# A fused RWKV-5 attention and SoLU block: zeros, own products, scalings and one join on other engines or in another order, and the decay rates loaded as eight rows

## The chip, the cores and the metric

The kernel runs on one core of a Trainium2 chip. Times are device microseconds (us) of one execution. A core has five engines that run side by side: TensorE (PE, with its weight loads shown apart as PEld), VectorE (DVE), ScalarE (ACT), GpSimd (POOL) and SyncE (SP), which here does nothing but issue transfers. Each works through its own instructions in the order in which they were written, and waits for another only through semaphores. Sixteen DMA engines move data between the device's memory and the on-chip buffers SBUF and PSUM.

## What is computed

The first part is a linear attention with a decaying state, over 4 batches, 8 heads, 768 steps and 48 columns to a head; the second a feed-forward block with the activation SoLU on its 3072 rows.

```python
# attention: r, k, v (4, 8, 768, 48); w, u (8, 48)
for t in range(S):
    cur = einsum('bhd,bhe->bhde', u[None] * k_t, v_t)
    y[:, :, t] = einsum('bhd,bhde->bhe', r_t, state + cur)
    state = w[None, :, :, None] * state + einsum('bhd,bhe->bhde', k_t, v_t)
# x: y as (4*768, 8*48); w_in (384, 1024), w_out (1024, 384)
h = x @ w_in
solu = h * softmax(h)
ln = (solu - mean(solu)) / sqrt(var(solu) + 1e-6) * g_ln
out = ln @ w_out
```

The weights w_in, w_out and g_ln are read in single precision or as the words of doubles, which the kernel turns into single precision itself ("convert" below).

## The kernel before

The 768 steps of each batch are cut into six chunks of 128, so there are 24 units of 128 rows, taken batch by batch within a chunk: unit i is batch i mod 4 of chunk i // 4. A unit goes through the attention, then through w_in (two units later, `LA`), and then through w_out (five units after that, `LO`). The order of the instructions on every engine is the order of the program text: `direct_path` turns automatic scheduling off. The other path in the file, `general_path`, is only taken when a check at the end (decay rates and sums within bounds) fails.

**The start.** SP issues the loads of k, r, v and of the pieces of w_in in the written order (lines 594 to 608). ACT's queue carries only two small loads, w (L493) and u (L496). The 8 x 48 decay rates go to four rows of `wq`, with two heads in each, padded with ones to 64 columns, and PE turns them into `wd_ps`, 128 x 4 (L636). From these DVE builds the powers in `tab` by doubling: `back` and `fore`. PE turns `back` into `kd_ps`, and ACT copies that to `kdec` (L665), the factors of the keys. u goes to one row, and PE spreads it over 128 rows through `u_ps`, which ACT copies to `u_bc` (L639). Right behind that copy ACT fills the second half of each of the six v buffers with zeros (L641), 128 x 512 each.

Then a list written out by hand (lines 1313 to 1396) brings in the first units. `turn_r` and `turn_k` turn r and k by PE; DVE multiplies with `fore` (L779) and, for unit 0, with `back` (L790). `decay_k` is POOL's product of k and kdec (L721). `weigh` forms u times k (L734) and times r (L735), both on POOL, and DVE's `sum_own` (L739) adds these up to the own term of each row and head. `diagonal` puts that on the diagonal of the score matrix: for the first four units ACT does so in eight pieces (L749), for the later ones POOL (L754). `take_scores` is DVE's masked copy of the scores from PSUM (L827, later L832); `whole_y`, `merged_y` are PE's products with v. `spin` is a filler product of PE. The state is advanced by `outer` and `whole_outer` (PE), `middle` and `update` (DVE).

**The pieces of the weights.** There are 14: six of w_in and eight of w_out. `convert_a` (ACT, L537), `convert_b` (two operations of DVE, L550 and L552) and `convert_c` (POOL, L560) build the single-precision words. `convert_d` multiplies a piece of w_out with the negative of g_ln: on ACT if the flag `scalar` is set (L568), else on DVE (L571). In the loop of lines 1399 to 1448 the odd pieces go to ACT and the even ones to DVE. In each of its passes the order on ACT is: exponential of `h_ps` (L977), copy of the turned keys, `convert_a`, the two operations of `unit_b`, `convert_d`, then (in the last two passes) `halve_ln`, `place` (L771, L772), the copy of y (`take_y`, L892). On DVE it is: `turn_r`'s product (L779), `unit_a` (L1049, L1053, which reads h_ps and so frees it), `convert_d`, the own sums, state, scores, and `convert_b`.

**The feed-forward.** `ffn_in` multiplies with w_in (L969). `unit_a` forms solu, `unit_b` the sum of squares. `variance`, `root` and `shifts` make the two numbers to a row with which `normalise` (ACT, L1102) scales a unit. `halve_ln` splits the words into halves of 16 bits, SP transposes them by DMA (L1116), and DVE's `join_ln` joins the halves again (L1121). `row_sums_12` and `row_sums_34` (L1201 to L1207) form sums for a scheme that needs seven products where eight are usual; `both_a` to `both_d` are its products with w_out (L1211) and the copies of their results. At the end the last unit's `shifts` run on DVE, between two joins:

```python
    both_c(l)
    shifts(i, N, nc.vector)
    join_ln(l + 3)
    row_sums_12(l + 2)
```

Of the kernel before, what the change touches and what calls it, by code (L numbers as in the profile page):

```python
# [9 lines left out]
F32 = mybir.dt.float32  # L10
# [389 lines left out]
def direct_path(  # L400
# [29 lines left out]
    nc = tc.nc  # L430
    B, H, S, D = r.shape
    T = 128
    P = U = 64
    C = S // T
    HP = H // 2
# [13 lines left out]
    const = ctx.enter_context(tc.tile_pool(name="const", bufs=1))  # L449
    apool = ctx.enter_context(tc.tile_pool(name="apool", bufs=2))  # L450
# [15 lines left out]
    NLD, NV = 5, 6  # L466
    rpads = [const.tile([128, H, P], F32, name=f"rpad{i}") for i in range(NLD)]
    kpads = [const.tile([128, H, P], F32, name=f"kpad{i}") for i in range(NLD)]
    vts = [const.tile([128, 2, H, P], F32, name=f"vt{i}") for i in range(NV)]
# [12 lines left out]
                    in_=v[b, :, ds(c * T + at, size), :].rearrange("h s d -> s h d"))  # L482


    wq = const.tile([HP, 2, P], F32, name="wq")
    u_bc = const.tile([128, H, D], F32, name="u_bc")
    g_sb = const.tile([128, KF], F32, name="g_sb")
    minus_g = const.tile([128, KF], F32, name="minus_g")
# [1 line left out]
    w_out_sb = const.tile([128, KF, dm], F32, name="w_out_sb")  # L490
    decays = const.tile([128, HP], F32, name="decays")

    nc.scalar.dma_start(out=wq[:, :, 0:D], in_=w.rearrange("(a q) d -> a q d", q=2))  # L493
    nc.vector.memset(wq[:, :, D:], 1.0)
    u_row = u_bc[0:1].rearrange("p h d -> p (h d)")
    nc.scalar.dma_start(out=u_row, in_=u.rearrange("h d -> (h d)").unsqueeze(0))  # L496
    for i in range(NLD):
# [42 lines left out]
    def convert_b(j):  # L540
        hi, low = step[j]
        n = low.shape[1]
        ma = wpool.tile([128, n], U32, tag="ma", name="ma", bufs=4)
        part = ma
        if pieces[j][2] is None:
            part = psM.tile([128, n], F32, tag="m", name="part").bitcast(U32)

        nc.vector.tensor_scalar(out=part, in0=hi, scalar1=3, scalar2=0x3FFFFFF8,  # L550
                                op0=ALU.logical_shift_left, op1=ALU.bitwise_and)
        nc.vector.scalar_tensor_tensor(out=ma, in0=hi, scalar=0xC0000000, in1=part,  # L552
                                       op0=ALU.bitwise_and, op1=ALU.bitwise_or)
        step[j] = ma, low
# [8 lines left out]
    def convert_d(j, scalar=False):  # L563
        dst, _, f = pieces[j]
        ma, low = step.pop(j)
        if f is not None:
            if scalar:
                nc.scalar.activation(out=dst, in_=ma.bitcast(F32), func=ACT.Copy,  # L568
                                     scale=minus_g[:, f : f + 1])
            else:  # L570
                nc.vector.tensor_scalar_mul(out=dst, in0=ma.bitcast(F32),  # L571
                                            scalar1=minus_g[:, f : f + 1])
# [37 lines left out]
    ident = const.tile([128, 128], F32, name="ident")  # L610
# [22 lines left out]
    pw = const.tile([128, 2, 8, HP], F32, name="pw")  # L633
    nc.vector.memset(back[:, :, T - 1 : T], 1.0)
    wd_ps = psM.tile([128, HP], F32, tag="m", name="wd_ps")
    nc.tensor.transpose(wd_ps, wq.rearrange("a q d -> a (q d)"), ident[0:HP, 0:HP])  # L636
    u_ps = psM.tile([128, dm], F32, tag="m", name="u_ps")
    nc.tensor.matmul(u_ps, ones_row, u_row, start=True, stop=True)
    nc.scalar.copy(out=u_bc.rearrange("p h d -> p (h d)"), in_=u_ps)  # L639
    for vt in vts:  # L640
        nc.scalar.activation(out=vt[:, 1].rearrange("p h x -> p (h x)"),  # L641
                             in_=ident[:, 0:1].to_broadcast([128, H * P]), func=ACT.Copy, scale=0.0)
    nc.vector.tensor_scalar(out=pw[:, 0, 0], in0=wd_ps, scalar1=LOW, scalar2=HIGH,
# [64 lines left out]

    ones = const.tile([128, 1], F32, name="ones")
    nc.gpsimd.memset(ones, 1.0)  # L710

    live = {}

# [4 lines left out]
    def decay_k(i):  # L718
        X = live.setdefault(i, {})
        X["kp"] = apool.tile([128, H, P], F32, name="kp", bufs=5)  # L720
        nc.gpsimd.tensor_mul(X["kp"].rearrange("p h d -> p (h d)"),  # L721
                             kpads[i % NLD].rearrange("p h d -> p (h d)"),
                             kdec.rearrange("p a d -> p (a d)"))
# [5 lines left out]
                             rpads[i % NLD].rearrange("p h d -> p (h d)"),  # L729
                             rdec.rearrange("p a d -> p (a d)"))  # L730

    def weigh(i, engine):
        rku = live[i]["rku"] = apool.tile([128, H, D], F32, name="rku")
        engine.tensor_mul(rku, kpads[i % NLD][:, :, 0:D], u_bc)  # L734
        engine.tensor_mul(rku, rku, rpads[i % NLD][:, :, 0:D])  # L735

    def sum_own(i):
        own = live[i]["own"] = small.tile([128, H, 1], F32, name="own")
# [35 lines left out]
    def turn_r(i):  # L774
        rT = factors(i)["rT"]
        ps = psM.tile([128, HP, T], F32, tag="m", name="tr_ps")
        for a in range(HP):
            nc.tensor.transpose(ps[:, a, :], pair(rpads[i % NLD], a), ident)
        nc.vector.tensor_mul(rT, ps, fore)  # L779
# [287 lines left out]
    def unit(i):  # L1067
        unit_a(i)
        unit_b(i)
# [9 lines left out]
    def shifts(i, j, engine):  # L1079
        i = max(i, SEVEN)  # L1080
        if i < j:
            tot, shift, scale, rstd = (stats[:, n, i:j] for n in (1, 2, 3, 4))
            engine.tensor_scalar(out=scale, in0=rstd, scalar1=-float(dff), scalar2=1.0,
                                 op0=ALU.mult, op1=ALU.mult)
            engine.tensor_tensor(out=shift, in0=tot, in1=rstd, op=ALU.mult)  # L1085
# [34 lines left out]
    def join(words, turned):  # L1120
        nc.vector.tensor_copy(out=words.bitcast(U16).rearrange("p n (t o) -> p o n t", o=2),  # L1121
                              in_=turned)
# [7 lines left out]
    def join_ln(i):  # L1130
        X = live[i]
        if i not in ROOM:
            X["lnT"] = fpool.tile([128, KF, 128], F32, name="lnT")
        else:
            X["lnT"] = bigs[ROOM[i]].rearrange("p (f t) -> p f t", f=KF)
        join(X["lnT"], X["turned"])
# [72 lines left out]
    def block(dst, rows, weights, start=False):  # L1209
        for f in range(KH):  # L1210
            nc.tensor.matmul(dst, rows[:, f], weights[:, f], start=(start and f == 0),  # L1211
                             stop=(f == KH - 1), skip_group_check=True)
# [52 lines left out]
    def both_c(i):  # L1265
        X, Y = live.pop(i), live.pop(i + 1)
        ending[i] = X
        o, o2, a, e = (X[n] for n in ("o", "o2", "a", "e"))
        rows, rows2 = (out[ds(b * S + c * T, T)] for b, c in (units[i], units[i + 1]))
        if not X.get("summed"):  # L1270
            nc.vector.tensor_tensor(out=o2[:, right], in0=a, in1=o2[:, right], op=ALU.add)
        block(a, Y["lnT"][:, KH:KF], sums_w[4])
        if i + 2 == N:
            nc.sync.dma_start(out=rows2[:, right], in_=o2[:, right])
        if X.get("summed") != 2:
            nc.vector.tensor_tensor(out=o[:, right], in0=e, in1=o[:, right], op=ALU.add)
        nc.sync.dma_start(out=rows, in_=o)
# [13 lines left out]
    def attend(chunks, at=0):  # L1291
        chunks = [i for i in chunks if i < N]
        scores(chunks, at)
        outer(chunks)
# [25 lines left out]
    for q in range(2):  # L1320
        rows = slice(q * P, q * P + D)
        nc.gpsimd.tensor_tensor(out=wide.rearrange("p (a q) -> p a q", q=2)[P : P + D, :, q],
                                in0=back[rows, :, 0], in1=pw[rows, 0, 0], op=ALU.mult)
    weigh(0, nc.gpsimd)
    decay_k(0)
    sum_own(0)
    diagonal(0)
# [1 line left out]
    spin(2)  # L1329
    whole_scores(0)  # L1330
    convert_b(0)
    decay_k(1)
    weigh(1, nc.gpsimd)
    turn_r(1)
    spin(4)
# [63 lines left out]
    for i in range(LA, LA + LO):  # L1399
        j = i - LA  # L1400
        load(i + 5, "kr")
        load(i + 4, "v")
        if i > LA:
            ffn_in(j)
        before, now = now, [todo.pop(0) for _ in range(2 if todo else 0)]
        turn_r(i + 2)
        turn_k(i + 2)
        for p in before:
            convert_c(p)
        for p in now:  # L1410
            take_up(p)
        if i > LA:
            diagonal(i + 1)
            unit(j)
        for p in before:
            convert_d(p, p % 2)
        sum_own(i + 2)
        decay_k(i + 3)
        if i + 3 >= FIRST:
            decay_r(i + 3)  # L1420
        weigh(i + 3, nc.gpsimd)
        if i - LO >= 0:
            halve_ln(i - LO)
        if i - LO - 1 >= 0:
            join_ln(i - LO - 1)
        if i + 1 < WHOLE:
            whole_scores(i + 1)
            take_scores(i + 1)
        else:
            place(i + 1)  # L1430
            attend([i + 1])
            middle(i + 1)
        if LA < i < WHOLE:
            whole_y(i)
            take_y(i)
            whole_outer(i)
        elif i >= WHOLE:
            merged_y(i)
            take_y(i)
        if i > LA:  # L1440
            update(i)
        else:
            nc.vector.tensor_single_scalar(out=minus_g, in_=g_sb, scalar=-1.0, op=ALU.mult)
        if i + 1 >= WHOLE:
            take_scores(i + 1)
        for p in now:
            convert_b(p)
        halve_rk(i + 3)
# [17 lines left out]
    i = LA + LO  # L1466
    j, l = i - LA, 0
# [41 lines left out]
    for i in range(LA + LO + 2, ELEVEN, 2):  # L1509
        j, l = i - LA, i - LA - LO  # L1510
# [8 lines left out]
        first, second = ([n] if n < N else [] for n in (i + 2, i + 3))  # L1519
# [121 lines left out]
    for i in range(ELEVEN, N - 1, 2):  # L1641
        j, l = i - LA, i - LA - LO
        one, two = turned[i]
        first, second = ([n] if n < N else [] for n in (i + 2, i + 3))
# [80 lines left out]
    i = N - 1  # L1725
    j, l = i - LA, i - LA - LO
# [68 lines left out]
    variance(i, N, nc.vector)  # L1795
    root(i, N)
    both_c(l)
    shifts(i, N, nc.vector)
    join_ln(l + 3)
    row_sums_12(l + 2)  # L1800
    row_sums_34(l + 2, nc.vector)
    both_d(l)
# [72 lines left out]
```

## Time and profile before

| | us |
|---|---|
| median of three runs | 322.94 |
| the three runs | 321.37, 322.94, 323.55 |
| the profiled execution | 322.73 |
| its span | 321.0 |

| engine | busy, us | share of the span | instructions |
|---|---|---|---|
| PE | 307.4 | 96% | 3903 |
| PEld | 216.9 | 68% | 3903 |
| DVE | 265.9 | 83% | 449 |
| ACT | 244.4 | 76% | 418 |
| POOL | 245.6 | 77% | 264 |

Busy time is from the first table of the page. The span is the time from the first to the last recorded instruction; what is outside it is the launch. The chain of waits is followed back from the last instruction to what released it, step by step; a line of it gives a start, a duration and an instruction. A line of the timeline gives start and duration in us, engine, line of the program, operation, written and read buffers with their partitions and elements, how often it runs without a break, and, in brackets, the idle time of the engine before it and what ended it. A row that merges several instructions gives their joint length.

### The profile page before, as it was taken

To read this page: it belongs to the slowest core of one execution; us is meant where nothing else is said; L and a number is where in the kernel's file an instruction comes from. 1 tells how busy PE (TensorE), PEld (TensorE's weight loads), DVE (VectorE), ACT (ScalarE), POOL (GpSimd) and SP (SyncE) were. 2 spreads that over 40 slices of the span, in tenths; PEclk is the share of its full clock that TensorE was granted. 3 is DMA by queue.
4 is the path that set the end of the run, shared out by engine and by line. 5 is a ranking of instruction groups with operands and counts; after the bars stand their busy time and mean duration, and the time that the engine had idled before them with its cause. 6 is when DMAs were issued, how large, how long until landed. Compare 5 with 4: busy or idle time off the path is not lost.

```text
span 321.0 us, 9696 instructions
## 1 busy us (share of the span) xinstructions
PE 307.4 (96%) x3903; PEld 216.9 (68%) x3903; DVE 265.9 (83%) x449; ACT 244.4 (76%) x418; POOL 245.6 (77%) x264
## 2 busy tenths in 40 slices
PE   6989999999999999999999999999999999999992
PEld 4866566555456466687677677678768677769891
DVE  7796999998887988989889799799979946777760
ACT  3875888888559888968968969959959968788420
POOL 3999778889999999999999999979988274272000
PEclk9999999999999999999999999999999999999998
DMA  7999998778999999988999999995876445675912
GB/s 161 241 266 208 200 188 205 119 142 134 190 170 178 173 175 150 162 145 169 165 196 180 168 191 209 197 196 114 143 174 144 85 121 118 135 191 116 204 76 61
DMA packets 165780, 52.64 MB, mean 164 GB/s; under 512 B 158301, under 2 KB 161502, under 8 KB 165726
## 3 DMA queue, kind: packets, MB, share of 16 engines
q1 hardware_dynamic: 165712, 51.92, 83.3%
q8 instruction: 33, 0.54, 0.7%
q14 instruction: 21, 0.17, 0.2%
q10 hardware_dynamic: 14, 0.00, 0.0%
HBM read 26.75 MB, written 4.72 MB: 98 GB/s over the span
## 4 chain that ended last, share of the span: by engine, by line
PE 61%; POOL 18%; DVE 10%; issue 4%; DMA 3%; SPq 1%; ACT 0%; POOLq 0%; ACTq 0%
PE o_ps L1211 26%; PE h_ps L969 16%; PE h_part L1003 9%; POOL kp L721 4%; POOL rku L734 4%; POOL big L754 3%; POOL rp L728 3%; PE y_ps L881 2%; POOL rku L735 2%; PE at L819 2%; DMA vt<-in_v_dram 1%; DVE ma L552 1%; PE h_part L881 1%; DMA wq<-in_w_dram 1%; DVE big L832 1%
## 5 line engine op out<-in xcount | busy, mean ns | idle before, releaser
L969 PE MATMUL h_ps<-w_in_sb,xT 128*128 128x512 f32 x216 | 96.9, 598 | 0.0
L969 PEld LDWEIGHTS h_ps<-w_in_sb,xT 128*128 128x128 f32 x216 | 39.9, 190 | 44.9 <-issue 43.2
L1127 ACT COPY halves<-solu 128x2048 uint16<-128x2048 uint16 x23 | 43.6, 1895 | 1.9 <-DMA halves<-halves 1.7
L721 POOL TENSOR_TENSOR kp<-kpad,kdec 128x512 f32<-128x512 f32 x24 | 34.1, 1423 | 0.9 <-ACT kdec L665 0.2
L1121 DVE COPY big<-halves 128x2048 uint16<-128x2048 uint16 x21 | 33.8, 1613 | 0.6 <-DMA halves<-halves 0.3
L1121 DVE COPY lnT<-halves 128x2048 uint16<-128x2048 uint16 x18 | 31.2, 1759 | 0.0
L735 POOL TENSOR_TENSOR rku<-rku,rpad 128x384 f32<-128x384 f32 x24 | 29.2, 1218 | 1.9
L832 DVE COPY_PREDICATED big<-later_half,at 64x512 f32<-64x512 uint32 x40 | 29.5, 736 | 0.7
L734 POOL TENSOR_TENSOR rku<-kpad,u_bc 128x384 f32<-128x384 f32 x24 | 29.8, 1241 | 0.2
L754 POOL TENSOR_SCALAR_AFFINE_SELECT big<-own 64x512 f32<-64x512 f32 x40 | 27.6, 691 | 1.8
L1211 PE MATMUL o_ps<-w_out_sb,ma 128*128 128x192 f32 x160 | 28.1, 328 | 0.0
L1211 PEld LDWEIGHTS o_ps<-w_out_sb,ma 128*128 128x128 f32 x160 | 26.2, 190 | 1.9 <-issue 1.6
L728 POOL TENSOR_TENSOR rp<-rpad,rdec 128x512 f32<-128x512 f32 x15 | 25.1, 1674 | 0.0
L977 ACT ACTIVATE e<-h_ps 128x1024 f32<-128x1024 f32 x18 | 18.4, 1022 | 8.7 <-PE h_ps L969 8.6
L1061 ACT ACTIVATE e<-solu,stats 128x1024 f32<-128x1024 f32 x20 | 23.0, 1148 | 2.2 <-DVE solu L1053 2.1
L1053 DVE SCALAR_TENSOR_TENSOR solu<-h_ps,stats,e 128x1024 f32<-128x1024 f32 x18 | 23.1, 1284 | 1.5
L1102 ACT ACTIVATE solu<-solu,stats 128x1024 f32<-128x1024 f32 x17 | 21.0, 1233 | 1.0 <-POOL stats L1085 0.9
L1166 PE MATMUL o_ps<-w_out_sb,lnT 128*128 128x384 f32 x64 | 21.6, 491 | 0.0
L1072 POOL TENSOR_SCALAR stats<-stats 128x2 f32<-128x2 f32 (+2 forms) x13 | 5.9, 451 | 19.2 <-ACT e L1061 18.7
L956 POOL TENSOR_TENSOR vt<-vt,wide 48x384 f32<-48x384 f32 x16 | 19.4, 1226 | 0.8
L1211 PE MATMUL o_ps<-w_out_sb,lnT 128*128 128x192 f32 x112 | 19.8, 330 | 0.0
L1211 PEld LDWEIGHTS o_ps<-w_out_sb,lnT 128*128 128x128 f32 x112 | 18.2, 190 | 1.7 <-issue 1.4
(198 smaller groups left out, 699.2 us busy)
## 6 DMA issues: line engine op xcount, KB each, us to landing
raw<-in_moe_w_out_dram SPq DMA_DIRECT2D x16, 384.0 KB, 4.1
kpad<-in_k_dram SPq DMA_DIRECT2D x24, 192.0 KB, 5.1
rpad<-in_r_dram SPq DMA_DIRECT2D x24, 192.0 KB, 5.0
vt<-in_v_dram SPq DMA_DIRECT2D x40, 96.0 KB, 3.6
raw<-in_moe_w_in_dram SPq DMA_DIRECT2D x7, 512.0 KB, 6.7
out_dram<-o SPq DMA_DIRECT2D x18, 192.0 KB, 3.0
raw<-in_moe_w_in_dram SPq DMA_DIRECT2D x10, 256.0 KB, 3.8
out_dram<-kp SPq DMA_DIRECT2D x5, 192.0 KB, 2.5
```

The costliest lines, as they stand in the source:

```text
L721: nc.gpsimd.tensor_mul(X["kp"].rearrange("p h d -> p (h d)"), kpads[i % NLD].rearrange("p h d -> p (h d)"), kdec.rearrange("p a d -> p (a ...
L728: nc.gpsimd.tensor_mul(X["rp"].rearrange("p h d -> p (h d)"), rpads[i % NLD].rearrange("p h d -> p (h d)"), rdec.rearrange("p a d -> p (a ...
L734: engine.tensor_mul(rku, kpads[i % NLD][:, :, 0:D], u_bc)
L735: engine.tensor_mul(rku, rku, rpads[i % NLD][:, :, 0:D])
L754: nc.gpsimd.affine_select(out=G[rows, c].rearrange("p a q u -> p (a q) u"), in_=X["own"][rows].to_broadcast([U, H, U]), compare_op=ALU.is_ ...
L832: nc.vector.copy_predicated(X["G"][rows, c].rearrange("p a q u -> p q a u"), later_half[rows].unsqueeze(1).to_broadcast([U, 2, HP, U]), X[ ...
L969: nc.tensor.matmul(h_ps[:, ts(n, NX)], X["xT"][:, j, :], w_in_sb[:, j, ts(n, NX)], start=(j == 0), stop=(j == KD - 1))
L1003: nc.tensor.matmul(dst, rows, weights, start=start, stop=True, skip_group_check=True)
L1053: nc.vector.scalar_tensor_tensor(out=solu, in0=X["h"], scalar=rs, in1=X["e"], op0=ALU.mult, op1=ALU.mult, accum_out=tot)
L1121: nc.vector.tensor_copy(out=words.bitcast(U16).rearrange("p n (t o) -> p o n t", o=2), in_=turned)
L1127: copy(out=both.rearrange("p (o n) -> p o n", o=2), in_=split(X["solu"]))
L1211: nc.tensor.matmul(dst, rows[:, f], weights[:, f], start=(start and f == 0), stop=(f == KH - 1), skip_group_check=True)
```

## The change

Five things are changed.

1. `wq` has eight rows, one for each head, and w is loaded as it lies in memory. Two products with every second column of the identity matrix, for even and for odd heads, take the place of one turn.
2. ACT writes zeros to the first four v buffers only. POOL writes them to the other two, behind its constant `ones`.
3. `weigh` can put its second product on another engine; for unit 0 that is DVE. `decay_k(1)` stands ahead of `decay_k(0)` on POOL, instead of behind the conversion of the first piece.
4. `convert_d` is always on ACT in the loop.
5. In the ending one `join_ln` stands ahead of the last unit's `shifts` on DVE.

```diff
-    wq = const.tile([HP, 2, P], F32, name="wq")
+    wq = const.tile([H, P], F32, name="wq")
...
-    nc.scalar.dma_start(out=wq[:, :, 0:D], in_=w.rearrange("(a q) d -> a q d", q=2))
-    nc.vector.memset(wq[:, :, D:], 1.0)
+    nc.scalar.dma_start(out=wq[:, 0:D], in_=w)
+    nc.vector.memset(wq[:, D:], 1.0)
...
-    nc.tensor.transpose(wd_ps, wq.rearrange("a q d -> a (q d)"), ident[0:HP, 0:HP])
+    for q in range(2):
+        nc.tensor.matmul(wd_ps[ts(q, P)], wq, ident[0:H, q:H:2], start=True, stop=True)
...
-    for vt in vts:
+    for vt in vts[:4]:
         nc.scalar.activation(out=vt[:, 1].rearrange("p h x -> p (h x)"),
                              in_=ident[:, 0:1].to_broadcast([128, H * P]), func=ACT.Copy, scale=0.0)
...
     nc.gpsimd.memset(ones, 1.0)
+    for vt in vts[4:]:
+        nc.gpsimd.memset(vt[:, 1], 0.0)
...
-    def weigh(i, engine):
-        rku = live[i]["rku"] = apool.tile([128, H, D], F32, name="rku")
+    def weigh(i, engine, second=None):
+        rku = live.setdefault(i, {})["rku"] = apool.tile([128, H, D], F32, name="rku")
         engine.tensor_mul(rku, kpads[i % NLD][:, :, 0:D], u_bc)
-        engine.tensor_mul(rku, rku, rpads[i % NLD][:, :, 0:D])
+        (second or engine).tensor_mul(rku, rku, rpads[i % NLD][:, :, 0:D])
...
-    weigh(0, nc.gpsimd)
+    weigh(0, nc.gpsimd, nc.vector)
+    decay_k(1)
     decay_k(0)
...
     convert_b(0)
-    decay_k(1)
     weigh(1, nc.gpsimd)
...
         for p in before:
-            convert_d(p, p % 2)
+            convert_d(p, True)
...
     both_c(l)
+    join_ln(l + 3)
     shifts(i, N, nc.vector)
-    join_ln(l + 3)
     row_sums_12(l + 2)
```

## The prediction

> **What bounds the kernel now.** First the waits of TensorE and the busy time by stretch, then the chain of waits, then the timeline around each edited line. Busy time by stretch, in us:
>
> ```profile
> 0.00:23.40 23.40, 18.95 (x288) 15.65 (x288) 18.56 (x60) 15.21 (x35) 17.47 (x35) 1.00 0.93 224
> ...
> 50.00:76.00 26.00, 24.39 (x413) 14.12 (x403) 24.85 (x45) 22.85 (x39) 22.00 (x22) 1.00 0.75 139
> 76.00:130.00 54.00, 53.68 (x649) 31.83 (x648) 46.28 (x57) 41.86 (x62) 51.84 (x49) 1.00 1.04 170
> ```
>
> Columns: stretch, length, then busy PE, PEld, DVE, ACT, POOL, the clock, DMA, GB/s. From 23.4 (the first h_ps product) to 298.5 PE lacks only some 3 us: 1.6 in 50 to 76, 0.3 near 128, 0.5 near 213, 0.55 near 298. So an edit pays only by bringing 23.4 forward or closing one of these gaps. After 298.5 PE is followed to the end, so what is gained before it is kept. The chain through the start:
>
> ```profile
> 8.46 1.01 POOL rku L734
> 9.54 1.00 POOL rku L735
> 10.54 0.17 issue
> 10.74 2.52 POOL kp L721 x2
> 13.26 0.96 POOL rku L734
> 14.30 1.02 POOL rku L735
> ```
>
> Start, us, what. GpSimd does own products and decayed keys one after another. DVE's sum of own products of chunk 1 starts only at 15.35, and DVE then runs without a break until the scores of chunk 1 are taken (18.62), for which PE waits. The timeline of ACT and POOL there:
>
> ```profile
> 6.97 3.22 ACT L641 ACTIVATE vt<-ident 128x512 f32<-128x512 f32 x6
> ...
> 10.09 0.57 ACT L665 COPY kdec<-kd_ps 128x512 f32<-128x512 f32 x1
> ...
> 10.74 2.52 POOL L721 TENSOR_TENSOR kp<-kpad,kdec 128x512 f32<-128x512 f32 x2 [0.20 <-ACT kdec L665]
> ```
>
> The copy of kdec stands behind six zero writes although PE has kd_ps ready at 8.25 + 1.06 = 9.31.
>
> **What the Trainium skill says.** "ScalarE: Activation LUTs" (What ACT_TABLE_LOAD costs): 186 ns + 0.833 ns per element, 93 ns more for a pointer operand, and neighbours overlap by 93 ns. That is 613 ns for a 512-element zero and 599 for a 384-element scaling; the trace has 617 and 600. "VectorE: DVE Perf Modes" (The TRN2 errata): an fp32 product of two tensors takes (N+151)/0.96 ns; 691 ns at 512, and the row sums L1201 show 0.69. "SBUF — State Buffer" (Who interferes with whom): a DVE instruction with two SBUF inputs, or a copy using both ports, and a GpSimd instruction that reads SBUF lock each other out for a whole instruction. The trace agrees: the join at 69.55 takes 1.96 us, against 1.32 alone, as POOL's kp runs to 70.32, and POOL's rp behind it takes 2.33 instead of 1.24. "DMA: Bandwidth & Descriptors" (Why a DMA increments its semaphore by 16 and not by 1): a transfer is spread over the most engines, up to 16, that divide its slowest dimensions: four for w now, eight then. No view of this trace shows that split.
>
> **Part 1, the load of w.** It is issued at 0.79 on ACT's queue, holds the issue for 1.27 us, and its product starts at 4.38. Two products (48 of 64 useful columns, 4 wide) replace the turn of 0.24 us; one more costs about 0.1, the pitch of small matmuls here. This shifts the tables by 0.1, without effect: PE reaches the turn of the table (8.04) after u_ps, tr_ps and tk_ps, and the table is ready at 7.78. The transfer: never later than now by more than 0.3 (a second way of spreading 1.5 KB); earlier by up to 1.0, if the issue shrinks to the 0.27 of u's, as u follows on the same queue (2.10) and gates ACT (4.88) and u_ps. I take 0; the other end is a rival.
>
> **Part 2, zeros.** Two of six leave ACT: at the pitch of 0.54, ACT is free at 6.97 + 4 x 0.54 = 9.1, so kdec's copy starts with kd_ps, 9.4, and ends at 9.95 instead of 10.66. POOL gets two zero writes of 512 elements. No row has them: at least 0.3 (128 elements take 0.19), at most 1.3 (its 512-element product takes 1.28); I take 0.6. POOL is idle from 3.9 to 7.94, so 1.2 costs nothing, and even 2.6 would end at 6.5. Without that cover wide and everything behind would slip by the excess.
>
> **Part 3, own products of chunk 0, order of the decays.** POOL drops one product of 1.00. It ends the first at 9.46 and waits for kdec: decay_k(1) at 10.05 instead of 10.74. DVE takes the second, (384+151)/0.96 = 0.56 us, into its idle 1.39 us before 10.57: 9.55 to 10.1, and sums at 10.1 instead of 10.57. By the lock it may hold POOL's decay back by 0.1. So POOL gains 0.6 to 0.7, not the whole 1.0, since kdec is late next. decay_k(0) moves behind decay_k(1) and ends at 12.7; only the outer product of chunk 0 waits for it (PE at 15.47). weigh(1) ends at 14.65 instead of 15.31, the sum comes 0.65 earlier, and so do DVE's unbroken run, the scores and the first h_ps. The transfers don't come earlier. The fourth w_in piece lands at about 19.0 (issue at 12.38, 6.6 to landing), ACT takes it at 19.70; the sixth lands near 22.6 and is taken at 23.05. Those slacks are 0.7 and 0.45, so 0.65 of gain just fits (the second delays ACT by 0.2, with 0.45 to spare before DVE needs that diagonal). I take **-0.65**, with -0.3 and -0.75 as ends.
>
> **Part 4, scalings.** Four of 0.46 to 0.64 us (mean 0.55) leave DVE, four of 0.60 go to ACT; the queue of SP is not passed. On ACT they delay place, the copy of y and the next exponential. ACT waits 1.0, 0.70, 0 and 0 us ahead of the next four exponentials, but in the third and fourth passes 0.88 and 1.15 ahead of unit_b, a wait for DVE's solu. On DVE, 0.55 earlier, the product L779 frees the bank for which PE waits 0.66 twice (57.4, 66.6). First gap: 0.5 is won. But the exponential at 66.05 is bound by ACT itself: unit_b 0.5 earlier, 0.6 added, so it is 0.1 later. solu and with it the h_ps product at 68.86 wait for it, which returns the 0.5. The next slip (0.7 at 75.46) lies under o_ps (75.56 to 81). Left over: 0.3 at 74.57, less 0.1 to 0.2: **-0.15**, ends -1.4 (all gaps gone) and +1.2 (two uncovered scalings). POOL's conversions, which wait 6.6 us for DVE in eight places, come up to 1 us sooner, and the 0.3 gap at 128.38, which hangs on POOL through the own sums at 121.11, partly closes: **-0.2**, ends 0 and -0.5.
>
> **Part 5, join ahead of shifts.** At the end PE stands still before 298.51:
>
> ```profile
> 294.70 0.35 DVE L1276 TENSOR_TENSOR kp<-o_ps,kp 128x192 f32<-128x192 f32 x1
> 294.86 0.55 POOL L1076 TENSOR_TENSOR stats<-stats,neg_half 128x1 f32<-128x1 f32 x1 [3.73 <-DVE stats L1072]
> ...
> 295.45 0.15 DVE L1083 TENSOR_SCALAR stats<-stats 128x1 f32<-128x1 f32 x1 [0.40 <-POOL stats L1076]
> ...
> 295.58 1.32 DVE L1121 COPY big<-halves 128x2048 uint16<-128x2048 uint16 x1
> ```
>
> DVE idles 0.40 for POOL's root. The join can start at 295.05 (its turned factors landed near 292.5), and the row sums come up to 0.35 sooner. But the shifts then end at 296.6 instead of 295.67; ACT's normalise waits for them, and behind it stand the copy of the left block (297.63) and halve_ln. ACT is busy until 296.4 anyway, so it slips 0.15 to 0.2, and PE would start at about 298.15. By the lock, the join may wait for the root: then nothing is won, and ACT slips 0.5. Ends -0.4 and +0.2; I take **-0.2**.
>
> **Sum.** 0.65 + 0.15 + 0.2 + 0.2 = 1.2 us less than the profiled execution (322.73, span 321.0 and 1.7 around it): 321.5. The median of the runs shown is 0.2 above that execution, within their spread of 2.2, so I leave 321.5.
>
> **Rivals.** (a) The mechanism above, 321.5, own range 320.6 to 322.3: chance 0.50. (b) w and u land about 1 us earlier. For: 1.27 against 0.27 us of issue on one queue; PE waits 1.3 and DVE 1.0 for it. Against: the first issue of the queue may cost this in any form, and DVE's memsets last to 3.66, so at most 0.95 is won ahead of the tables. The start then wins 1.6 instead of 0.65 (kdec at 9.0, second key landed 8.55): 320.5; with all gaps closed too, 319. Chance 0.27. (c) The start's gain is swallowed by landing transfers (DMA 0.93 to 1.05 busy) and the scalings cancel: 322.7, chance 0.13. (d) Slower: ACT becomes the bound between 60 and 76. It decides where ACT's wait before unit_b falls below the added 0.6; if it does in all four passes, 2.4 us are added, less 0.85 from start and end: 324.3. For: no idle time before the exponentials at 66.05 and 75.46. Against: DVE is the busier engine there, 24.85 against 22.85 of 26. Chance 0.10. That w is still on four engines and nothing in part 1 changes is contained in (a).
>
> **Numbers.** Likeliest 321.5; eight in ten between 319.4 and 323.2, which takes in (b), (c) and the ends of parts 4 and 5. One per cent, about what a measurement of this kernel can tell from no change, is 3.2 us: faster than 319.7 needs (b) with the gaps of part 4 closed, 0.21; slower than 326.2 needs more than (d), 0.04; within, 0.75.
>
> **What would show it.** kdec's copy near 9.4, decay_k(1) near 10.05, own sums at 10.1 and 14.7, the first h_ps near 22.7: part 3 right. wd_ps below 3.8: (b). The h_ps product 9.2 us after its predecessor as now (59.62 to 68.86), and ACT without a wait before it: part 4 right; 8.6 us: underrated. The last stage's join at 295.05 relative to now, or only after the root: part 5. Wrong if the first h_ps moves by less than 0.3, or more than 1.2, or a new PE gap over 0.5 us stands between 76 and 290.

## The result, and the profile after

The changed kernel takes 320.41 us (median of 12 runs, 319.2 to 321.59), the kernel before 322.76 beside it (12 runs). The ratio is 0.993, with an interval of 0.9911 to 0.9948: 2.3 us less, inside the predicted range and within one per cent, and 1.1 us below the predicted 321.5. Rival (b), an earlier landing of w and u, had put it at 320.5. The profiled execution took 321.01, its span 319.3.

Where does the time go? The start of PE's products at a few fixed places of the program, in us from the start of the span, gives the account. "w alone" and "all but w" are two of the experiments below.

| start of | before | after | w alone | all but w |
|---|---|---|---|---|
| the first h_ps product | 23.33 | 21.38 | 21.67 | 22.34 |
| h_ps, second pass of the loop | 50.45 | 48.98 | 49.11 | 49.60 |
| h_ps, end of the third pass | 68.86 | 67.52 | 67.49 | 68.86 |
| h_ps behind the gap near 128 | 129.76 | 127.72 | 128.40 | 128.70 |
| the block behind the last gap | 298.51 | 296.29 | 296.32 | 297.39 |
| DVE's last copy | 314.85 | 312.64 | | |
| end of the span | 321.0 | 319.3 | 318.4 | 319.7 |

1.95 us are gained ahead of the first h_ps product; 0.5 of it is lost by 49 and 0.1 more by 67.5, and 0.9 is won from there on, mostly ahead of 128 and at the end. Of the 2.2 us at the last copy the span shows 1.7: the issue of the last output takes 1.09 us in this execution, against 0.69 before.

Two of these steps need care. PE has a gap that the profile calls "issue" shortly ahead of the first h_ps product:

```profile
21.63 0.30 PE L858 MATMUL y_ps<-big,vt 128*32 128x128 f32 x2 [0.73 <-issue]
...
19.66 0.31 PE L861 MATMUL y_ps<-big,vt 128*32 128x128 f32 x4 [0.35 <-issue]
```

The first line is from before, the second from after: 0.38 of the 1.95 us is this difference, and the gap comes and goes in the runs below, whatever their edit. A second one, at 213.86, cost 0.47 before and is missing in the changed kernel and in "w alone". That is why "w alone", which has gained 1.36 by 129, stands level with the changed kernel at 296: 0.7 of its 2.19 there is won across this gap.

Busy time by stretch of the kernel after: stretch, length, then busy PE, PEld, DVE, ACT, POOL, the clock, DMA share and GB/s. The stretches are those of the prediction, cut at the same places of the program:

```profile
0.00:21.40 21.40, 18.25 (x291) 14.92 (x291) 18.80 (x60) 14.27 (x32) 17.01 (x36) 1.00 0.97 234
21.40:49.00 27.60, 27.58 (x427) 16.93 (x425) 24.47 (x45) 21.90 (x49) 22.99 (x23) 1.00 1.01 198
49.00:74.00 25.00, 23.80 (x377) 13.66 (x374) 22.74 (x40) 23.08 (x41) 21.78 (x23) 1.00 0.84 145
74.00:126.40 52.40, 52.28 (x641) 30.63 (x641) 43.53 (x55) 41.28 (x59) 50.39 (x46) 1.00 1.02 174
```

The first stretch is 2 us shorter, with more transfer per us (0.97 of the DMA engines, against 0.93). In the third ACT is now the busier of the two, 23.08 against DVE's 22.74; PE still lacks 1.2 there. In the fourth it lacks 0.1.

The start, first two lines of the kernel before:

```profile
0.79 1.27 ACTq L493 DMA_DIRECT2D wq<-in_w_dram  x1
...
4.38 0.24 PE L636 MATMUL wd_ps<-ident,wq 4*128 4x4 f32 x1 [1.33 <-DMA wq<-in_w_dram]
```

Then the timeline of the kernel after:

```profile
0.79 0.60 ACTq L493 DMA_DIRECT2D wq<-in_w_dram  x1
1.42 0.23 ACTq L496 DMA_DIRECT2D u_bc<-in_u_dram  x1
2.99 0.38 PE L637 MATMUL wd_ps<-ident,wq 8*64 8x4 f32 x4
3.84 1.01 POOL L713 MEMSET vt<- 128x512 f32 x2
6.10 2.18 ACT L642 ACTIVATE vt<-ident 128x512 f32<-128x512 f32 x4
8.47 0.59 ACT L666 COPY kdec<-kd_ps 128x512 f32<-128x512 f32 x1 [0.19 <-PE kd_ps L665]
8.58 0.56 DVE L738 TENSOR_TENSOR rku<-rku,rpad 128x384 f32<-128x384 f32 x1 [0.27 <-POOL rku L737]
9.14 2.52 POOL L724 TENSOR_TENSOR kp<-kpad,kdec 128x512 f32<-128x512 f32 x2 [0.59 <-ACT kdec L666]
13.76 0.55 DVE L742 TENSOR_REDUCE own<-rku 128x8 f32<-128x384 f32 x1 [0.43 <-POOL rku L738]
```

Issuing the load of w holds ACT's queue for 0.60 us where it held it for 1.27, and u follows at 1.42 instead of 2.10. The product with w starts at 2.99 instead of 4.38, without waiting for the transfer: no bracket names it. DVE's tables start at 3.52, where before they waited until 4.66. The packets of ACT's queue show the landing itself: those of w run from 2.86 to 3.14 before and from 1.75 to 1.85 after, and u's follow at 3.75 and 2.86. Of the 1.3 us, 0.67 is the shorter issue; the rest lies between the end of the issue and the first packet, 0.80 before and 0.36 after. What follows has the forecast's order, 1.4 to 1.6 us earlier than before and 0.9 earlier than the forecast: the zeros on POOL (0.5 each) end long before POOL is needed, kdec's copy now follows PE (before, it ran behind the zeros), and the decay follows that copy. The chain of waits agrees. Its pieces (start, us, what) no longer alternate between own products and decays of POOL, but go through one own product and then to DVE and ACT:

```profile
3.11 0.48 DVE at L504
...
7.54 1.01 POOL rku L737
8.58 0.57 DVE rku L738
9.18 0.57 DVE own L742
9.77 2.17 ACT big L752 x7
```

PE's waits over the whole execution (line, what it waited for: us in total, times, longest us):

```profile
PE u_ps L639 <- DMA u_bc<-in_u_dram: 0.7, 1, 0.7
PE y_ps L884 <- ACT big L791: 0.7, 1, 0.7
PE o_ps L1214 <- DVE lnT L1124: 0.7, 1, 0.7
...
PE kv_ps L916 <- DVE big L782: 0.3, 1, 0.3
PE o_ps L1214 <- ACT kp L1231: 0.2, 1, 0.2
```

Before, this list had 1.3 for w, twice 0.66 for DVE's `big` in the loop, and 0.6 for DVE at the end. Now PE waits for u, for ACT's copy of the turned keys (L791) in the loop, and 0.2 for ACT at the end. The 0.7 for `lnT`, at 215.16, is hardly a part of the change, since of the twelve experiments below one shows it. It cost something all the same: at 213.86 the changed kernel was 2.72 ahead (it lacks the gap that stood there before), at 215 it was 1.95 ahead.

New in the kernel after are waits for transfers in the first two passes. Timeline of ACT and POOL:

```profile
22.30 0.68 ACT L537 ACTIVATE lows<-raw 128x512 uint32<-128x512 uint32 x1 [0.84 <-DMA raw<-in_moe_w_in_dram]
...
33.02 1.28 POOL L724 TENSOR_TENSOR kp<-kpad,kdec 128x512 f32<-128x512 f32 x1 [0.88 <-DMA kpad<-in_k_dram]
...
48.66 0.56 ACT L537 ACTIVATE lows<-raw 128x384 uint32<-128x384 uint32 x1 [0.53 <-DMA raw<-in_moe_w_out_dram]
```

The engines now run up to the data: the sixth piece of w_in, keys, a piece of w_out. That the 0.5 us between 21 and 49 are lost by this is argued, not shown: PE loses them in pieces of 0.1 to 0.2 (at 30.2, 39.1 and 47.5) without a marked wait, and the last of the three waits comes after that. In three experiments below PE itself waits for a converted piece of w_in, 0.2 us each time.

The end, in the timeline:

```profile
292.97 1.47 POOL L1079 TENSOR_TENSOR stats<-stats,neg_half 128x1 f32<-128x1 f32 x1 [3.73 <-DVE stats L1075]
293.07 1.33 DVE L1124 COPY big<-halves 128x2048 uint16<-128x2048 uint16 x1
...
294.47 0.15 DVE L1086 TENSOR_SCALAR stats<-stats 128x1 f32<-128x1 f32 x1
...
294.61 0.68 DVE L1204 TENSOR_TENSOR ma<-big 128x512 f32<-128x512 f32 x1
...
296.29 0.92 PE L1214 MATMUL o_ps<-lows,ma 128*128 128x192 f32 x4 [0.23 <-ACT kp L1231]
```

The join no longer waits for the root. The root waits for the join: it lasts 1.47 instead of 0.55 and ends when the join does, though its recorded start is 0.10 us the earlier one. All seven runs with this order show the same.

### The profile page after: what moved, and what is told of

It reads as the page before. It is cut to its first block, busy times and chain, and to the rows that moved or that the text cites. A ratio compares the mean times of both kernels' runs of the same rounds, so it can differ in the third digit from the quotient of the medians.

```text
span 319.3 us, 9704 instructions
## 1 busy us (share of the span) xinstructions
PE 307.2 (96%) x3906; PEld 216.1 (68%) x3906; DVE 263.9 (83%) x446; ACT 246.0 (77%) x420; POOL 245.2 (77%) x265
## 4 chain that ended last, share of the span: by engine, by line
PE 58%; POOL 16%; DVE 16%; issue 4%; DMA 1%; ACT 1%; SPq 1%; POOLq 0%; ACTq 0%
PE o_ps L1214 26%; PE h_ps L972 15%; PE h_part L1006 8%; POOL rp L731 3%; POOL rku L737 3%; POOL big L757 3%; POOL kp L724 3%; DVE ma L552 2%; PE at L822 2%; PE y_ps L884 2%; POOL rku L738 2%; DVE lnT L1124 2%; DVE big L830 1%; DVE solu L1056 1%; DVE own L742 1%
## 5 line engine op out<-in xcount | busy, mean ns | idle before, releaser
L1124 DVE COPY lnT<-halves 128x2048 uint16<-128x2048 uint16 x18 | 30.3, 1698 | 0.8 <-DMA halves<-halves 0.8
L737 POOL TENSOR_TENSOR rku<-kpad,u_bc 128x384 f32<-128x384 f32 x24 | 28.8, 1201 | 0.2
L1075 POOL TENSOR_SCALAR stats<-stats 128x2 f32<-128x2 f32 (+2 forms) x13 | 4.7, 365 | 18.8 <-ACT e L1064 18.1
```

## The experiments

The question is what the additional 1.1 us are. The theory is that w and u arrive over 1 us earlier because the destination of the load has no gap in its rows, and that this adds to the forecast's sum; for the rest that sum stands. Against it stand: u matters rather than w (order on the queue); the number of rows matters rather than the gap; the forecast undervalued the zeros and the order, the scalings or the join. Ratios are to the kernel before on the same chip, with 95% intervals; where a single execution is named, only its trace counts.

### Part 1 alone

```diff
-    wq = const.tile([HP, 2, P], F32, name="wq")
+    wq = const.tile([H, P], F32, name="wq")
...
-    nc.tensor.transpose(wd_ps, wq.rearrange("a q d -> a (q d)"), ident[0:HP, 0:HP])
+    for q in range(2):
+        nc.tensor.matmul(wd_ps[ts(q, P)], wq, ident[0:H, q:H:2], start=True, stop=True)
```

> Only part 1 of the change (w as eight rows, two products). Theory 1 (w and u land about 1 us earlier and set the start): w's issue 0.6 us, its product near 3.0, kdec's copy still behind six zeros but these start 0.9 earlier, so at 9.35; first decayed key near 10.0 instead of 10.74, first h_ps near 22.6 (23.33 before), time 0.5 to 0.9 us less. Theory 2 (the gain of the start comes from the zeros and the order of the decays, the load of w is worth nothing): first h_ps at 23.2 to 23.4, time the same within 0.2 us.

Measured: 321.01 us, ratio 0.9955 (0.9934 to 0.9977), 1.45 us less. The issue takes 0.60, the product starts at 2.98, kdec's copy at 8.92 and the decay at 9.57, both 1.17 earlier than before. In the timeline of ACT, the first line from before and the others from this run:

```profile
4.88 1.28 ACT L639 ACT_TABLE_LOAD   x1 [4.88 <-DMA u_bc<-in_u_dram]
...
3.71 1.28 ACT L640 ACT_TABLE_LOAD   x1 [3.71 <-DMA u_bc<-in_u_dram]
...
5.80 3.22 ACT L642 ACTIVATE vt<-ident 128x512 f32<-128x512 f32 x6
...
8.92 0.57 ACT L666 COPY kdec<-kd_ps 128x512 f32<-128x512 f32 x1
```

ACT's wait for u ends 1.17 earlier. Behind it stand, in both kernels, 0.43 of waiting for u's product, then u's copy, the six zeros and kdec's copy without idle time. With six zeros on ACT it is thus u's landing, behind w on the queue, that sets kdec's copy; kd_ps itself is ready by 8.14. DVE's own sum of chunk 1 is at 14.18 instead of 15.35, the same 1.17; the first h_ps product is 1.66 earlier. The 0.5 that the last stage adds is a gap of PE that the profile puts down to "issue", 0.73 before and 0.25 here, among the last y_ps products ahead of it. This part alone gives more than the forecast gave to the whole change, and more than the 0.5 to 0.9 expected of it here.

### All but part 1

The reverse of that diff on the changed kernel.

> The changed kernel with w loaded and turned as before (part 1 undone). Theory 1: the start wins only the 0.65 us of the forecast, first h_ps near 22.7, time 1.2 us less than before, so about 1.1 more than the changed kernel. Theory 2: first h_ps near 21.4 as in the changed kernel, time about 2.3 us less than before.

Measured: 321.44 us, ratio 0.9967 (0.9959 to 0.9975), 1.05 us less; forecast without a gain from part 1: 1.2. kdec's copy at 9.46 (forecast 9.4), decay at 10.13 (10.05), own sums at 9.85 and 14.74 (10.1 and 14.7), first h_ps product at 22.34 (22.7). The forecast's sum is right for what it valued, but not its path: of the 0.99 won at the first h_ps product nothing is left at 68.86, where ACT's copies are late (0.30 and 0.69), and the 1.06 at 129 is won behind that, 0.4 at 74.6 and most of the rest at the gap near 128. In the time of the runs the two parts add up within the intervals, 1.45 + 1.05 = 2.5 against 2.3. At the first h_ps product they don't: 1.66 + 0.99 = 2.65 against 1.95.

### u ahead of w

The kernel before with its two small loads exchanged.

```diff
+    u_row = u_bc[0:1].rearrange("p h d -> p (h d)")
+    nc.scalar.dma_start(out=u_row, in_=u.rearrange("h d -> (h d)").unsqueeze(0))
     nc.scalar.dma_start(out=wq[:, :, 0:D], in_=w.rearrange("(a q) d -> a q d", q=2))
     nc.vector.memset(wq[:, :, D:], 1.0)
-    u_row = u_bc[0:1].rearrange("p h d -> p (h d)")
-    nc.scalar.dma_start(out=u_row, in_=u.rearrange("h d -> (h d)").unsqueeze(0))
```

> The kernel before, with u's load issued ahead of w's. If the first transfer of ACT's queue costs 1.27 us in any form: u's issue takes about 1.3, w's about 0.3. If the form of w's load costs it: u's issue about 0.25 at 0.79, w's about 1.27 behind it, w's product near 4.6. Time within 0.3 us of before either way.

Measured in a single execution (323.11 us): the timeline of this run.

```profile
0.79 0.53 ACTq L494 DMA_DIRECT2D u_bc<-in_u_dram  x1
1.36 0.76 ACTq L495 DMA_DIRECT2D wq<-in_w_dram  x1
...
5.36 0.24 PE L636 MATMUL wd_ps<-ident,wq 4*128 4x4 f32 x1 [2.30 <-DMA wq<-in_w_dram]
```

u took 0.27 as the second load and takes 0.53 as the first; w took 1.27 as the first and takes 0.76 as the second. Neither expectation holds alone: as the second load w still takes half a microsecond more than u, which belongs to its form, and being the first costs w 0.5 and u 0.3. w's product starts at 5.36, 1 us later than before, and the first h_ps product at 23.60. This does not clear u: it has landed by 2.21, but PE turns to it only behind w's product, at 5.47. PE takes u behind w in every run, so what each of the two landings is worth is not separated; both come earlier with the one change.

### Four plain rows instead of eight

The kernel before with w as four rows of 96 values without a gap; the ones of the padding are written to `wd_ps` by DVE instead.

```diff
-    wq = const.tile([HP, 2, P], F32, name="wq")
+    wq = const.tile([HP, 2, D], F32, name="wq")
...
-    nc.scalar.dma_start(out=wq[:, :, 0:D], in_=w.rearrange("(a q) d -> a q d", q=2))
-    nc.vector.memset(wq[:, :, D:], 1.0)
+    nc.scalar.dma_start(out=wq.rearrange("a q d -> a (q d)"), in_=w.rearrange("(a q) d -> a (q d)", q=2))
...
-    nc.tensor.transpose(wd_ps, wq.rearrange("a q d -> a (q d)"), ident[0:HP, 0:HP])
+    nc.vector.memset(wd_ps, 1.0)
+    for q in range(2):
+        nc.tensor.matmul(wd_ps[q * P : q * P + D], wq[:, q], ident[0:HP, 0:HP], start=True, stop=True)
```

> The kernel before, with w still in four rows, but each row one stretch of 96 values without a gap at the destination (the padding is written by DVE into PSUM instead). If the number of rows, and so of DMA engines, sets issue and landing: issue about 1.2 us, w's product near 4.3. If the gap at the destination sets it: issue 0.3 to 0.7, w's product at 3.0 to 3.8.

```profile
0.79 0.56 ACTq L493 DMA_DIRECT2D wq<-in_w_dram  x1
...
3.64 0.06 DVE L635 MEMSET wd_ps<- 128x4 f32 x1
...
3.76 0.32 PE L637 MATMUL wd_ps<-ident,wq 4*48 4x4 f32 x4 [0.70 <-DVE wd_ps L635]
```

The issue takes 0.56: as little as with eight rows. But the product waits 0.70 for the ones, which stand behind DVE's other memsets, so its start (a single execution, 322.2 us, first h_ps at 22.86) doesn't tell when w landed. The same with the ones written early, right behind the load:

> The kernel before with w in four rows without a gap, as the earlier run, but the padding written by DVE ahead of everything, so that it hides nothing. If the gap at the destination is the whole difference: issue about 0.56, w's product near 3.0 as with eight rows, first decayed key near 9.6, first h_ps near 21.7. If the number of rows also counts: product at 3.4 or later.

```profile
0.79 0.55 ACTq L493 DMA_DIRECT2D wq<-in_w_dram  x1
...
2.98 0.33 PE L637 MATMUL wd_ps<-ident,wq 4*48 4x4 f32 x4
```

The product starts at 2.98, as with eight rows, and the first h_ps product at 21.50 (eight rows: 21.67); a single execution, 321.6 us. The 2.98 alone would prove little, since PE waits for no transfer there but for a write of DVE, in both. The packets decide: those of w end at 1.80 in both kernels with four plain rows, at 1.84 to 1.88 in the six with eight rows, and at 2.94 to 3.14 in the five that load w first and with the gap. So four or eight rows make no difference; the form with the gap does. Nor is it the number of pieces, since before and with eight rows w is eight packets of 192 bytes. With the gap goes a third dimension in the load's pattern, at both ends; the two were not separated.

### Parts 2 and 3 alone

Zeros, own products and the order of the decays on the kernel before.

> Only parts 2 and 3 (two zero writes on POOL, second own product on DVE, order of the decays) on the kernel before. Forecast: kdec's copy near 9.4, first decayed key near 10.05, own sums near 10.1 and 14.7, first h_ps 0.65 sooner, near 22.7; time 0.6 to 0.8 us less. Rival (gain handed back, transfers late): first h_ps within 0.2 of 23.33.

Measured: 322.23 us, ratio 0.999 (0.9967 to 1.0012). The time expected was 0.6 to 0.8 less. Its w came 0.27 earlier than in the kernel before (product at 4.11). kdec's copy at 9.10 and the decay at 9.76 are 0.98 earlier, so 0.71 by the edit; own sums at 9.81 and 14.36. The first h_ps product, at 22.82, is only 0.51 earlier; PE again has an "issue" gap of 0.72 ahead of it. In the profile the step is there, in the time of the runs it can't be told from nothing.

### Part 4 alone

```diff
         for p in before:
-            convert_d(p, p % 2)
+            convert_d(p, True)
```

> Only part 4 (all eight scalings on ACT) on the kernel before. Theory 1 (ACT binds in the third and fourth of the four passes): the product of h_ps after the third pass starts where it did, 68.86, within 0.2, and a new wait of PE for ACT stands ahead of it, in place of the wait of 0.66 for DVE; time 0.0 to 0.4 us less. Rival (DVE was the bound, both waits go): h_ps near 67.8, time 0.8 to 1.4 us less. Rival (ACT not covered): h_ps at 69.4 or later, time 0.4 or more up.

Measured: 322.42 us, ratio 0.9985 (0.9961 to 1.0009). PE in the third pass, the first line from before and the others from this kernel:

```profile
67.27 0.57 PE L913 MATMUL kv_ps<-vt,kp 64*48 64x48 f32 x30 [0.66 <-DVE big L779]
...
66.31 0.92 PE L913 MATMUL kv_ps<-vt,kp 64*48 64x48 f32 x32 [0.18 <-ACT xT L892]
67.92 1.10 PE L881 MATMUL y_ps<-big,vt 112*32 112x64 f32 x64 [0.69 <-ACT big L788]
68.97 3.27 PE L969 MATMUL h_ps<-w_in_sb,xT 128*128 128x512 f32 x7
```

Before, PE waited 0.66 for DVE's `big` here and the h_ps product stood at 68.86. Now DVE is in time, and ACT's copy of the keys is late by 0.69: the product stands at 68.97, 0.1 later, as the forecast had it. Near 128 the gap is closed, and h_ps stands at 129.12 instead of 129.76.

### Part 5 alone

```diff
-    shifts(i, N, nc.vector)
     join_ln(l + 3)
+    shifts(i, N, nc.vector)
```

> Only part 5 (the join ahead of the shifts) on the kernel before. Theory 1 (the join takes DVE's idle time, POOL's root waits for the join): root about 1.5 us long instead of 0.55, PE's block at 298.5 starts 0.3 to 0.4 sooner; time 0.3 less, at the edge of what the rounds tell. Rival (the join waits for the root): block at 298.5 within 0.1, time the same.

Measured: 322.62 us, ratio 0.9994 (0.9973 to 1.0014), not to be told from nothing. In the timeline the root takes 1.46 us beside the join:

```profile
295.12 1.46 POOL L1076 TENSOR_TENSOR stats<-stats,neg_half 128x1 f32<-128x1 f32 x1 [3.74 <-DVE stats L1072]
295.21 1.33 DVE L1121 COPY big<-halves 128x2048 uint16<-128x2048 uint16 x1
...
298.43 1.24 PE L1211 MATMUL o_ps<-lows,ma 128*128 128x192 f32 x6 [0.23 <-ACT kp L1228]
```

From PE's block ahead (295.43, sixteen products) to the one behind the gap it takes 3.00 us, before 3.33, and with the whole change 3.00 as well: 0.33 gained. In this execution the start was 0.35 later by chance, so that 298.43 says nothing by itself.

### Even scalings back on DVE in the later two passes

If ACT binds there, DVE should have them again.

```diff
-            convert_d(p, True)
+            convert_d(p, i < LA + 3 or p % 2)
```

> The changed kernel, but in the third and fourth passes the even scaling stays on DVE as before. If ACT binds there: the wait of 0.69 of PE for ACT's copy of the keys at 65.8 goes or shrinks, h_ps at 67.52 comes 0.3 to 0.6 sooner, time 0.2 to 0.5 less than the changed kernel. If DVE binds instead: a wait of 0.6 for DVE's product comes back, h_ps within 0.1 of 67.52, time the same.

This helps nothing that can be told. 320.12 us, ratio 0.9925 (0.9897 to 0.9952), whose interval overlaps that of the changed kernel. The h_ps product of the third pass is at 67.83, not sooner than 67.52: PE waits 0.94 for DVE's `big` instead, and the gaps of 0.3 at 74 and near 128 are back: in this execution PE is 1.0 later at 127 than in the changed kernel. In the third pass the wait only changes its name between ACT and DVE.

### The changed kernel without part 4, and without parts 2 and 3

Two kernels that each take one part back.

> The changed kernel with the even scalings back on DVE in all four passes (part 4 undone). If part 4 is worth the 0.3 to 0.6 us seen by 129 us when it stands alone: the product of h_ps near 129 starts at 128.0 to 128.4 instead of 127.72, time 0.2 to 0.6 us above the changed kernel. If it is worth nothing beside an earlier start: 127.72 within 0.15, time the same.

Without part 4: 321.08 us, ratio 0.9946 (0.9927 to 0.9965). The waits for DVE's `big` are back, twice 0.7, and so is the one of 0.3 near 128; h_ps there stands at 128.26, where the changed kernel has 127.72. This execution had started sooner (first h_ps at 20.82), but PE then waited for the sixth piece of w_in and began the next h_ps product at 32.04 (changed kernel: 31.77).

> The changed kernel without parts 2 and 3 (all six zeros on ACT, both own products on POOL, decays in the old order). If the earlier w takes most of the start's gain for itself, because the later transfers let no more through: first h_ps near 21.6, time within 0.5 us of the changed kernel. If the parts add up as each alone (0.5 at the first h_ps): first h_ps at 21.9 or later, time 0.5 to 0.7 above the changed kernel.

Without parts 2 and 3: 321.12 us, ratio 0.9938 (0.992 to 0.9957). The timeline of PE in this kernel:

```profile
21.47 4.56 PE L970 MATMUL h_ps<-w_in_sb,xT 128*128 128x512 f32 x10
26.21 1.12 PE L970 MATMUL h_ps<-w_in_sb,xT 128*128 128x512 f32 x2 [0.18 <-POOL w_in_sb L560]
```

The first h_ps product is at 21.47, practically as in the changed kernel, and then stands still for the sixth piece; the next one is at 32.35 against 31.77. At 128 the difference is 0.48. So with w early, parts 2 and 3 bring no more than 0.5, since the transfers of w_in now limit the start. Both ratios overlap that of the changed kernel: the times alone don't separate these parts.

### The scalings of the third pass moved to the fourth

If ACT's added scalings hold PE up in the third pass, moving them should bring it forward.

```diff
-        for p in before:
-            convert_d(p, True)
+        if i == LA + 3:
+            held = before
+        else:
+            for p in (held if i == LA + 4 else []) + before:
+                convert_d(p, True)
```

> The changed kernel, but the two scalings of the third pass are done in the fourth, where the products of o_ps cover ACT. If ACT binds in the third pass: PE's waits of 0.16 and 0.69 ahead of 67.52 go, the exponential comes 1.1 us sooner, the product of h_ps at 66.7 to 67.0, time 0.3 to 0.8 us less than the changed kernel. Rival (the fourth pass binds then, or transfers and DVE take the place): o_ps at 73.85 within 0.2, time the same or up to 0.5 more.

```profile
66.62 5.42 PE L972 MATMUL h_ps<-w_in_sb,xT 128*128 128x512 f32 x12
...
73.76 2.52 PE L1169 MATMUL o_ps<-w_out_sb,lnT 128*128 128x384 f32 x7 [0.73 <-ACT xT L895]
```

h_ps comes at 66.62 instead of 67.52, so ACT's scalings were what PE waited for. But the next products then wait 0.73 for ACT's copy of y, which stands behind four scalings (L568 runs 2.12 us), and start at 73.76, in the changed kernel at 73.85. Time 320.72, ratio 0.9937 (0.9914 to 0.9961): the gain is handed straight back. So it doesn't matter in which of the two passes ACT does this work.

## Why the prediction was right, and where it fell short

The range held because it had been drawn to take in rival (b). The mechanism thought likeliest, (a), did not: 320.41 lies outside its own range of 320.6 to 322.3. Rival (b), with a chance of 0.27, has the time (320.5) and its sign, the product with w ahead of 3.8 (2.99).

- **Part 1, taken as 0 with ends +0.3 and -1.0:** this term was mis-sized. By itself it measured -1.45 (interval 0.7 to 2.1), and w landed 1.1 to 1.3 earlier. The prediction had the mechanism as rival (b), with 1.27 against 0.27 us of issue as its ground, and set against it that "the first issue of the queue may cost this in any form". The runs show that 0.3 (u, 0.53 against 0.27) to 0.5 (w, 1.27 against 0.76) belongs to being first, and not 1.0. It also held that at most 0.95 could be won ahead of the tables: it was 1.14 (4.66 to 3.52). That the Trainium skill ("DMA: Bandwidth & Descriptors", Why a DMA increments its semaphore by 16 and not by 1) lets the slowest dimensions set the number of engines was no help with the time: four plain rows served as well as eight. Its failing was to look at rows, where the gap inside a row counted.
- **Part 2:** right in size: the zeros took 0.5 each on POOL (estimated 0.6), in its idle time. Beside an early w they are not free, though: DVE's small copy into `tab` (L652, at 4.01) takes 0.39 instead of 0.17 while POOL writes them, and the tables are ready 0.2 later (6.86) than without parts 2 and 3 (6.65).
- **Part 3, -0.65:** right with part 1 left out: decay and second own sum are 0.61 earlier in "all but w", and 0.98 and 0.99 with these parts alone. In both runs w itself came 0.24 to 0.27 earlier than in the profile before, so the edit is worth 0.4 to 0.7 at the decay. How much of it reaches the end is less certain: in "all but w" the third pass hands the start's whole gain back, so that the agreement of the sum is in part luck. DVE's product took 0.56, as reckoned. The slack of 0.45 that the forecast gave the sixth piece of w_in is the one that ran out: with 1.95 gained, ACT waits 0.84 for it. This fits rival (c) as a cap on the larger gain, and part 3 bringing at most 0.5 beside part 1.
- **Part 4, -0.15 and -0.2:** right in kind. The first gap shrank from 0.66 to 0.28, the second passed to ACT, and h_ps followed its predecessor by 9.74 us (9.24 before). The sign given, 9.2, was not what its own working says: 0.5 won ahead of the predecessor and returned behind it makes 9.7 to 9.8, and the product itself 0.1 later, as in the run with part 4 alone. By 129 it brought 0.64 alone, and the changed kernel without it is 0.54 later there; forecast 0.35. Rival (d), ACT as the bound, came true in the third pass, where 0.5 of the gain went (1.84 ahead of it, 1.34 behind), and not in all four for 2.4.
- **Part 5, -0.2:** the gain was 0.33, just inside the end of 0.4. The fear that the join would wait for the root was wrong about the order. The join and the root lock each other out, as the Trainium skill ("SBUF — State Buffer", Who interferes with whom) has it, but here the root was the one to wait, 1.47 us instead of 0.55. That held the shifts back to 294.47 and with them ACT's normalise; PE's block waits for ACT's copy behind it, and 0.23 of the gap stays.
- **What would have made it wrong:** two of its own signs appeared, a first h_ps product more than 1.2 earlier and a PE gap over 0.5 between 76 and 290. The first is part 1. The second, 0.68 at 215, took back 0.8 that the gap at 213.86 in the profile before had given.

Open: PE's gaps of the kind "issue". The first stands ahead of y_ps products before the first h_ps product, 0.17 to 1.20 us in eleven of the fourteen profiled executions, the second near 213, 0.22 to 0.84 us in nine. It is each time the same product of PE's program, counted from its start (the 220th and the 2884th), whatever the edit, and it starts 1.3 to 1.6 us after a transfer of 16 KB on the queue that the profile calls "instruction" has ended. So PE probably waits for its own instructions there; no run tried that. Nor is it known why w lands later behind u (its packets run from 3.29 to 4.52, spread over 1.2 us where they took 0.3 as the first), or whether parts 2 to 5 singly shorten the runs: their 0.3 to 0.6 us show in traces only.

## What to carry to other kernels

Look at the issue time of a small load at the head of a kernel: compare the durations of the issues on one queue, and where one is several times its neighbour's, lay out its destination without gaps, though the arithmetic behind it then takes a few more instructions. Before valuing work moved from a busy engine to another, read who is second to arrive at the wait, since the gap passes to it. A start that is made faster is soon limited by the transfers that it runs into. And compare two profiles at many fixed places before you credit an edit with a step: here gaps of up to 1.2 us came and went that no edit had made.

## What the runs showed of the hardware

- The same 1.5 KB load, first on its queue, took 1.27 us of issue with a gap inside each destination row, and 0.55 to 0.60 without one, with four rows or eight. Its packets ended at 2.94 to 3.14 and at 1.80 to 1.88, and its consumer could start at 4.1 to 4.4 and by 2.98.
- Being the first load issued on the queue cost 0.3 to 0.5 us of issue: u took 0.53 as the first and 0.27 as the second (0.23 to 0.24 behind a plain w), w with the gap 1.27 and 0.76.
- A write of 128x512 zeros takes POOL about 0.5 us (1.01 for two). Beside it a DVE copy of 128x4 took 0.38 to 0.39 us in all four runs in which the two met, and 0.17 at the same place without it.
- A POOL operation on one element per row waits out a DVE copy that began beside it: 1.47 us instead of 0.55.
- PE stood still for up to 1.20 us at the same two places of its program in most executions, 1.3 to 1.6 us behind a 16 KB transfer of the instruction queue.
